# A sliding-window attention and Fourier mix: the two heads of a transposed score tile interleaved by row, so that one selection masks both

## The chip, the cores and the metric

The kernel runs on one core of one Trainium2 chip. The metric is the device time of one execution in microseconds (us); the kernel before and the changed kernel are each executed several times and the median is taken.

## The reference

Only `A_x` is used as the input of both branches (`B_x` is not read). Cut to what matters:

```python
# S = 2048 rows, D = 512, H = 32 heads of Dh = 16, window W = 256
x = A_x
g = sigmoid((x * gate_w).sum(-1, keepdims=True))

# branch a: Fourier mixing as real matrix products
a_ = x @ dft_hid_re.T ; b_ = x @ dft_hid_im.T
a  = dft_seq_re @ a_ - dft_seq_im @ b_

# branch b: causal attention over a sliding window of 256 keys
q, k, v = split_heads(x @ wqkv)
scores = (q @ k.T) * Dh ** -0.5
scores = where(0 <= i - j < W, scores, -1e9)
b = merge_heads(softmax(scores) @ v) @ wo

out = g * a + (1 - g) * b
```

## The kernel before

All products are taken in the type fp32r, and where full precision is wanted an operand is split into a high part `hi` and a rest `lo`, so that three matmuls stand for one product (`TERMS`).

**Attention.** The 32 heads are worked in 4 groups (`NG`) of 4 pairs (`NP`). A step `n` is one group and one block of 64 rows (`BQ`), so there are 4 x 32 = 128 steps (`N`). In `ring[0]` lie the queries and in `ring[1]` the keys of a group, all 2048 columns, with 96 partitions per pair and a few rows more for corrections. A matmul for one pair takes as its stationary operand a padded block, `pads[i][n % 2][:, p]`, 128 columns wide: `make_pad` copies 64 columns of the ring twice, each time multiplied by a column of `half` (1 in one head's partitions, 0 in the other's), so that columns 0 to 63 belong to head 0 of the pair and columns 64 to 127 to head 1.

- `s_pair(n, p)` (L346) forms the scores of 64 queries of both heads against up to 320 keys (`WIN`) in PSUM (tile name `s`), adds the mask and takes the row minimum on DVE (L358), then takes the exponential and its sum on ScalarE (L361). Only the minimum and the sum are kept.
- `t_pair(k, p)` (L426) runs `LAG` = 19 steps behind. It forms the transposed scores (tile name `t`): 64 keys of both heads on the partitions, up to 320 queries on the free axis, with the minimum already added by rows 96 to 99 of the operands. ScalarE takes the exponential into `pt` (L440). After every second pair GpSimd (POOL) sets the two ragged ends of the window to zero with affine selections: the first 64 columns (L445) and, for full windows, the last 64 (L449), for each head's 64 partitions by itself.
- `pv(n)` (L452) multiplies `pt` with `vpad`: for each pair 128 rows (64 keys of head 0, then 64 keys of head 1) by 32 columns, of which 16 belong to each head and the other 16 are zero. `v_load` (L406) brings the values of 4 steps from HBM into `vr`, `v_spread` (L416) copies them into the right quarter of `vpad` on POOL; the zeros were set once at the start (`clear_pads`, L203).
- `make_pad(0, ..)` runs on DVE for both heads, `make_pad(1, ..)`, the operand of `t_pair`, on DVE for head 0 (L339) and on ScalarE for head 1 (L337).

**Dense work.** The generator `dense()` yields matmuls of the projections (`dv`, `dqk`, `dab`) and of the two 2048 x 2048 products of the Fourier branch (`dc`, L518); `fill(n)` inserts them between the matmuls of the attention at a fixed rate, so that PE has work while DVE and ScalarE finish a score tile. DVE splits the DFT matrices as they arrive (L574, queued as `jobs`), DVE and ScalarE evict the PSUM tiles.

**Order.** PE's order is written out by hand (`manual_schedule`); the main loop at L836 sets which step of what stands where. `behind(...)` keeps some DVE, ScalarE and SP instructions in the order in which they are issued; the rest, POOL above all, is placed by a scheduler. Score tiles `s` and `t` share 4 PSUM buffers (`ps_a`): a matmul waits until the tile four places earlier was read by DVE (`s`) or by ScalarE (`t`). `pads[i]` has two buffers, `vpad` two, `vr` one.

**Start.** The first weights and the first quarter of x are split by DVE and ScalarE (L78 to L81, L157 to L159) before PE can form the first projection, while POOL builds the constants: `mask`, `ident`, `half`, `mrow`, the zero rows of `pads[0]` (L195) and of the rings (L191).

Of the kernel before, what the change touches and what calls it, by code (L numbers as in the profile page):

```python
# [7 lines left out]
F32 = mybir.dt.float32  # L8
F32R = mybir.dt.float32r
AF = mybir.ActivationFunctionType  # L10
OP = mybir.AluOpType
# [3 lines left out]
P = 128  # L15
# [5 lines left out]
BQ = 64  # L21
NB = S // BQ
WIN = 320
# [9 lines left out]
def fnet_window_mix(ctx: ExitStack, tc: tile.TileContext, xT, x, wqk, wv, wr, wi, cr, ci, wo, gw, out):  # L33
    nc = tc.nc

    const = ctx.enter_context(tc.tile_pool(name="const", bufs=1))
# [11 lines left out]
    v_scr = [dram.tile([2, P, 2, NG, 64], F32, name=f"v_scr{i}") for i in range(8)]  # L48
# [6 lines left out]
    def ld(dst, src):  # L55
        mark("sp", nc.sync.dma_start(dst, src))

    def f(ap):
        return ap.bitcast(F32)
# [4 lines left out]
    def mark(e, ins):  # L64
        last[e] = ins.ins

    @contextmanager
    def behind(*engines):
        with ExitStack() as es:
            for e in engines:  # L70
                if e in last:
                    es.enter_context(tc.issue_after(last[e]))
            yield
# [68 lines left out]
    with tc.manual_schedule(engines={mybir.EngineType.Activation, mybir.EngineType.DVE, mybir.EngineType.SP}):  # L142
# [12 lines left out]
        for dk in range(DK):  # L155
            c = slice(dk * 256, dk * 256 + 256)
# [7 lines left out]
    ring = [const.tile([P, NP, S], F32R, name=f"ring{i}") for i in range(2)]  # L164
# [3 lines left out]
    for h in (0, 64):  # L168
        m = mask[h:h + 64, :]
        nc.gpsimd.affine_select(m, m, pattern=[[1, WIN]], compare_op=OP.is_gt, fill=BIG,  # L170
                                base=0, channel_multiplier=-1)
        nc.gpsimd.affine_select(m, m, pattern=[[-1, WIN]], compare_op=OP.is_ge, fill=BIG,
                                base=256, channel_multiplier=1)
    ident = const.tile([P, P], F32R, name="ident")
    nc.gpsimd.memset(f(ident[:]), 1.0)
    nc.gpsimd.affine_select(ident[:], f(ident[:]), pattern=[[1, P]], compare_op=OP.is_equal, fill=0.0,
                            base=0, channel_multiplier=-1)

    half = const.tile([P, 2], F32, name="half")
    mrow = const.tile([P, 2], F32, name="mrow")  # L180
    for t, edges in ((half, ((0, 16, 32, 48, 64, 80), (16, 32, 48, 64, 80, 96))), (mrow, ((96, 98), (98, 100)))):
        nc.gpsimd.memset(t, 0.0)
        for h in range(2):
            for i, e in enumerate(edges[h]):
                a = t[:, h:h + 1]
                nc.gpsimd.affine_select(a, a, pattern=[[0, 1]], compare_op=OP.is_ge, fill=1.0 - i % 2,
                                        base=e - 1, channel_multiplier=-1)

    def clear_rows(i, ss):
        with behind("pool"):  # L190
            nc.gpsimd.memset(f(ring[i][96:128, :, ss * 512:(ss + 1) * 512]), 0.0)  # L191

    first_lo = f(XT[0, 0][96:128, 1]).rearrange("r (p c) -> r p c", p=NP)
    for t in pads[0]:
        mark("pool", nc.gpsimd.affine_select(t[96:128], first_lo, pattern=[[0, NP], [0, P]], compare_op=OP.is_gt,  # L195
                                             fill=0.0, base=0, channel_multiplier=0))
    clear_rows(1, 0)
    clear_rows(0, 0)
    vpad = [const.tile([P, 4, NP, 32], F32, name=f"vpad{b}") for b in range(2)]

    def clear_pads():
        for t in vpad:
            nc.gpsimd.memset(t, 0.0)  # L203
        for t in pads[1]:
            nc.gpsimd.memset(f(t[96:128]), 1.0)
            for h in range(2):
                a = t[96:128, :, 64 * h:64 * h + 64]
                nc.vector.tensor_scalar(a, f(a), mrow[96:128, h:h + 1], None, op0=OP.mult)


# [117 lines left out]
    def make_pad(i, n):  # L328
        if not 0 <= n < NG * NB:
            return  # L330
        t = pads[i][n % NPAD]
        b = n % NB
        with behind(*(("act", "dve") if n < NPAD else ())):
            for h in range(2):
                src, dst = f(ring[i][:96, :, b * BQ:(b + 1) * BQ]), t[:96, :, 64 * h:64 * h + 64]
                if i and h:
                    nc.scalar.activation(dst, src, AF.Copy, scale=half[:96, h:h + 1])  # L337
                else:
                    nc.vector.tensor_scalar(dst, src, half[:96, h:h + 1], None, op0=OP.mult)  # L339
        PAD[i, n] = t  # L340
# [65 lines left out]
    def v_load(n):  # L406
        if n >= NG * NB:
            return
        g, kb = divmod(n, NB)
        raw = at.tile([P, 4, 64], F32, name="vr", bufs=1)  # L410
        for h in range(2):
            ld(raw[64 * h:64 * h + 64].rearrange("r (c j) x -> r c j x", j=2),
               v_scr[kb // 4][:, :, h, g, :].rearrange("c (j r) x -> r c j x", r=64))
        VR[n] = raw

    def v_spread(n):  # L416
        if n >= NG * NB:
            return
        raw = VR.pop(n)
        v2 = vpad[n // 4 % 2]  # L420
        for h in range(2):
            r = slice(64 * h, 64 * h + 64)
            nc.gpsimd.tensor_copy(v2[r, :, :, 16 * h:16 * h + 16], raw[r].rearrange("r j (p d) -> r j p d", d=16))  # L423
        V2[n // 4] = v2

    def t_pair(n, p):  # L426
        q0 = n % NB * BQ
        w = min(WIN, S - q0)
        if p == 0:
            if "proj" in have:  # L430
                more.append(n)
            c = (n - more[0]) % 6 * NP * WIN if more else 3072
            if c + NP * WIN <= 3072:
                PT[n] = f(home[:, c:c + NP * WIN].rearrange("p (a b) -> p a b", a=NP))
            else:
                PT[n] = at.tile([P, NP, WIN], F32, name="pt", bufs=4)
        pt = PT[n]
        ps = ps_a.tile([P, 512], F32, name="t", tag="st")
        nc.tensor.matmul(ps[:, :w], PAD[1, n][:, p], ring[0][:, p, q0:q0 + w], start=True, stop=True)  # L439
        nc.scalar.activation(pt[:, p, :w], ps[:, :w], AF.Exp, scale=-1.0)  # L440
        if p % 2:
            ph = slice(p - 1, p + 1)
            for h in (0, 64):
                a = pt[h:h + 64, ph, 0:64]
                nc.gpsimd.affine_select(a, a, pattern=[[0, 2], [1, 64]], compare_op=OP.is_ge, fill=0.0,  # L445
                                        base=0, channel_multiplier=-1)
                if w == WIN:
                    a = pt[h:h + 64, ph, 256:320]
                    nc.gpsimd.affine_select(a, a, pattern=[[0, 2], [-1, 64]], compare_op=OP.is_gt, fill=0.0,  # L449
                                            base=0, channel_multiplier=1)  # L450

    def pv(n):  # L452
        g, kb = divmod(n, NB)
# [375 lines left out]
    def v_next(n):  # L829
        if n < N:  # L830
            for c in range(2):
                need(("v", n % NB // 2 + c))
            with behind(*(("sp",) if n < 8 else ())):
                v_load(n)

    for n in range(N + LAG + 1):  # L836
# [3 lines left out]
        if n == 7:  # L840
            clear_pads()
        k = n - LAG
        ring_ahead(n + 1)
        if k in (-1, 4):
            v_spread(0 if k < 0 else 4)
        if k in (-4, -1, 4):
            v_next({-4: 0, -1: 4, 4: 8}[k])
        if n == 0:
            make_pad(0, 0)
        for p in range(NP):  # L850
            if n < N:
                s_pair(n, p)
            fill(n)
            if 0 <= k < N:
                t_pair(k, p)
            if p == 0:
                make_pad(0, n + 1)
                if k >= -1:
                    make_pad(1, k + 1)
            fill(n)  # L860
            for at_n, at_p, do in TURN:
                u, j = divmod(n - at_n, 8)
                if p == at_p and j == 0 and 0 <= u < 16:
                    do(u)
            if p == 3 and k % 8 == 6 and 0 <= k < N:
                l_load(k // 8)
            if p == 0 and full:
                o_out()
            if p == 2 and (k - summed >= (5 if more else 3) or k == N):
                for j in range(summed, k):  # L870
                    pv(j)
                summed = k
            if p == 3 and 4 * spread - 5 < summed and 4 * spread < N and n >= fresh:
                v_spread(4 * spread)
                spread += 1
                v_next(4 * spread)
                fresh = n + 2
# [49 lines left out]
```

## Time and profile before

| what | value |
|---|---|
| time, median of 3 runs | 855.11 us (853.95 to 856.31) |
| profiled execution, its span | 854.1 us, 17219 instructions |
| PE matmul busy | 844.2 us, 99% of the span |
| DVE busy | 618.1 us, 72% |
| ScalarE (ACT) busy | 592.0 us, 69% |
| POOL busy | 372.6 us, 44%, 1067 instructions |
| DMA | 161.04 MB, mean 189 GB/s |

For the profiled execution the page gives the span, from its first to its last instruction, and no time beside it; the span lies 1.0 us below the median of the timed runs and within their range. In the page "busy" is the time in which an engine had an instruction under way; PE's matmuls are pipelined, so that a busy PE need not be at its peak. Each group's row reads: line, engine, operation, what it writes and reads with shapes, count, then busy us and mean ns of one, then the idle time of that engine just before these instructions and what ended most of it.

### The profile page before, as it was taken

How to read it: one execution, taken by the hardware profiler on the slowest of the kernel's cores; microseconds unless marked ns; L12 is line 12 of the kernel's file. 1: busy time of each engine (PE TensorE's matmuls, PEld its weight loads, DVE VectorE, ACT ScalarE, POOL GpSimd, SP SyncE). 2: the span in 40 equal slices, each digit the busy share in tenths (PEclk: the TensorE clock that was granted, in tenths of full speed). 3: DMA queues.
4: the chain of work that ended last, by engine and by line, in shares of the span. 5: the costliest groups of instructions: out<-in, count | busy, mean ns of one | idle time of the engine just before them, and what ended most of it. 6: DMA issues, size and time to landing. Idle time of an engine off the chain costs nothing.

```text
span 854.1 us, 17219 instructions
## 1 busy us (share of the span) xinstructions
PE 844.2 (99%) x5166; PEld 691.1 (81%) x5166; DVE 618.1 (72%) x2011; ACT 592.0 (69%) x1793; POOL 372.6 (44%) x1067
## 2 busy tenths in 40 slices
PE   8999999999999999999999999999999999999998
PEld 6788788788788888888878887788888887878876
DVE  5588978767879787669777787788988764447252
ACT  5388898888888987779778897678777765532020
POOL 9100254444542554555525555456355577830000
PEclk9999999999999999999999999999999999999999
DMA  7976577576665274444445447979784344339563
GB/s 240 289 234 201 177 253 239 203 240 216 205 233 188 52 221 129 145 121 151 138 133 143 158 150 228 267 264 298 246 232 136 119 154 133 130 119 289 148 188 133
DMA packets 94862, 161.04 MB, mean 189 GB/s; under 512 B 27312, under 2 KB 36272, under 8 KB 94768
## 3 DMA queue, kind: packets, MB, share of 16 engines
q1 hardware_dynamic: 94336, 159.28, 59.4%
q8 instruction: 40, 0.66, 0.3%
q10 hardware_dynamic: 432, 0.66, 0.2%
q14 instruction: 54, 0.44, 0.2%
HBM read 108.27 MB, written 51.64 MB: 187 GB/s over the span
## 4 chain that ended last, share of the span: by engine, by line
PE 92%; DVE 3%; DMA 3%; issue 1%; ACT 1%; SPq 0%; DVEq 0%; ACTq 0%
PE dc L518 40%; PE dab L294 10%; PE s L356 8%; PE t L439 8%; PE o L466 8%; PE dqk L271 8%; PE t L785 5%; PE dv L294 4%; DMA raw<-cr 1%; DMA raw<-xT 1%; DVE sm L358 1%; DMA pt<-wqk 1%; DVE pad L339 0%; DVE big L81 0%; DVE lo L574 0%
## 5 line engine op out<-in xcount | busy, mean ns | idle before, releaser
L361 ACT ACTIVATE sm<-sm,ml 128x320 f32<-128x320 f32 (+4 forms) x512 | 277.9, 544 | 102.7 <-DVE ml L358 97.3
L518 PE MATMUL dc<-big,hi 128*128 128x512 f32 x1020 | 344.1, 393 | 0.0
L358 DVE CUSTOM_DVE_ANT_0 sm<-s,mask 128x320 f32<-128x320 f32 (+4 forms) x512 | 235.3, 464 | 110.5 <-PE s L356 88.0
L445 POOL TENSOR_SCALAR_AFFINE_SELECT pt<-pt 64x128 f32<-64x128 f32 x392 | 136.1, 347 | 224.0 <-ACT pt L440 212.4
L518 PE MATMUL dc<-big,lo 128*128 128x512 f32 x510 | 200.5, 393 | 0.0
L518 PEld LDWEIGHTS dc<-big,hi 128*128 128x128 f32 x1020 | 179.7, 188 | 21.3
L440 ACT ACTIVATE pt<-t 128x320 f32<-128x320 f32 (+4 forms) x392 | 160.2, 411 | 43.5 <-PE t L439 41.1
L356 PE MATMUL s<-ring,pad 128*128 128x320 f32 (+4 forms) x512 | 157.7, 308 | 0.1
L439 PE MATMUL t<-ring,pad 128*128 128x320 f32 (+4 forms) x512 | 154.3, 301 | 0.4 <-DVE ml L358 0.4
L339 DVE TENSOR_SCALAR pad<-ring,half 96x256 fp32r<-96x256 f32 x384 | 119.8, 358 | 13.4 <-PE t L439 13.2
L449 POOL TENSOR_SCALAR_AFFINE_SELECT pt<-pt 64x128 f32<-64x128 f32 x344 | 121.7, 354 | 0.1
L356 PEld LDWEIGHTS s<-ring,pad 128*128 128x128 f32 x512 | 96.1, 188 | 30.2 <-issue 9.0
L439 PEld LDWEIGHTS t<-ring,pad 128*128 128x128 f32 x512 | 96.1, 188 | 22.4 <-DVE ml L358 1.6
L518 PEld LDWEIGHTS dc<-big,lo 128*128 128x128 f32 x510 | 95.9, 188 | 13.7 <-issue 1.6
L574 DVE TENSOR_TENSOR lo<-raw,hi 128x512 fp32r<-128x512 f32 x142 | 97.9, 698 | 0.1
L361 ACT ACTIVATION_READ_ACCUMULATOR sm<-sm,ml 128x1 f32 x512 | 97.5, 190 | 0.0
L294 PE MATMUL dab<-hi,big 128*128 128x512 f32 x256 | 89.1, 394 | 0.0
L271 PE MATMUL dqk<-big,hi 128*128 128x512 f32 x240 | 85.7, 394 | 1.3 <-DVE big L81 0.6
L423 POOL COPY vpad<-vr 64x256 f32<-64x256 f32 x64 | 26.9, 420 | 110.2 <-DMA vr<-v_scr 80.5
L574 DVE CAST hi<-raw 128x512 fp32r<-128x512 f32 x142 | 60.9, 438 | 17.4 <-PE dc L518 12.1
L445 POOL TENSOR_SCALAR_AFFINE_SELECT home<-home 64x128 f32<-64x128 f32 x120 | 45.1, 376 | 56.5 <-ACT home L440 49.0
L337 ACT ACTIVATE pad<-ring,half 96x256 fp32r<-96x256 f32 x128 | 63.8, 499 | 0.0
(96 smaller groups left out, 957.5 us busy)
## 6 DMA issues: line engine op xcount, KB each, us to landing
qk_scr<-home SPq DMA_DIRECT2D x32, 512.0 KB
ring<-qk_scr SPq DMA_DIRECT2D x32, 512.0 KB
raw<-cr SPq DMA_DIRECT2D x32, 512.0 KB
raw<-ci SPq DMA_DIRECT2D x32, 512.0 KB
r_scr<-ev SPq DMA_DIRECT2D x42, 256.0 KB
ev<-r_scr SPq DMA_DIRECT2D x42, 256.0 KB
ab_scr<-home SPq DMA_DIRECT2D x20, 512.0 KB
big<-ab_scr SPq DMA_DIRECT2D x20, 512.0 KB
```

What stands on the lines that cost most here:

```text
L271: nc.tensor.matmul(ps, w[a][:, c:c + 128], XT[dk, ss][:, b], start=n == 0, stop=n == 11)
L294: nc.tensor.matmul(ps, XT[dk, ss][:, a, c * 128:(c + 1) * 128], wh[b], start=n == 0, stop=n == 11)
L339: nc.vector.tensor_scalar(dst, src, half[:96, h:h + 1], None, op0=OP.mult)
L356: nc.tensor.matmul(ps[:, :w], PAD[0, n][:, p], ring[1][:, p, k0:k0 + w], start=True, stop=True)
L358: mark("dve", nc.vector.tensor_tensor_reduce(out=sm[:, :w], in0=ps[:, :w], in1=mask[:, WIN - w:], scale=1.0, scalar=3e38, op0=OP.add, op1= ...
L361: mark("act", nc.scalar.activation(sm[:, :w], sm[:, :w], AF.Exp, bias=nm[:, c], scale=-1.0, accum_out=l[:, c]))
L439: nc.tensor.matmul(ps[:, :w], PAD[1, n][:, p], ring[0][:, p, q0:q0 + w], start=True, stop=True)
L440: nc.scalar.activation(pt[:, p, :w], ps[:, :w], AF.Exp, scale=-1.0)
L445: nc.gpsimd.affine_select(a, a, pattern=[[0, 2], [1, 64]], compare_op=OP.is_ge, fill=0.0, base=0, channel_multiplier=-1)
L449: nc.gpsimd.affine_select(a, a, pattern=[[0, 2], [-1, 64]], compare_op=OP.is_gt, fill=0.0, base=0, channel_multiplier=1)
L518: nc.tensor.matmul(ps, w[a][:, i % 8 * 128:i % 8 * 128 + 128], ab[SC[i]][:, b], start=i == ends[0] and a + b == 0, stop=i == ends[1] and a ...
L574: return fn(*args)
```

## The change

In `pads[1]`, the operand of the transposed scores, the two heads of a pair no longer take columns 0 to 63 and 64 to 127 but alternate: column 2r + h is key r of head h. So the rows of `t` and `pt` alternate too, both heads' ragged ends lie in one pattern of rows and columns, and one affine selection over 128 partitions takes the place of two over 64. `make_pad(1, ..)` writes every second element on DVE and on ScalarE as before, in two instructions. The values have to follow: `v_load` fetches both heads' rows alternating with one DMA in place of two, and `v_spread` multiplies all 128 rows with a column that is 1 for one head's rows and 0 for the other's (`side`), so that the zeros of `vpad` are written each time and its clearing at the start goes. `side` is formed on DVE at the start from every second column of `ident`. The untransposed scores (`s`) keep their order.

```diff
@@ constants
+    side = const.tile([P, 2], F32, name="side")
 ...
+    nc.vector.reduce_sum(side[:, 0:1], f(ident[:]).rearrange("p (r h) -> p h r", h=2)[:, 0],
+                         axis=mybir.AxisListType.X)
+    nc.vector.tensor_scalar(side[:, 1:2], side[:, 0:1], -1.0, 1.0, op0=OP.mult, op1=OP.add)
+
+    def turned(t):
+        return t[:].rearrange("x p (r h) -> x p r h", h=2)
@@ clear_pads
-        for t in vpad:
-            nc.gpsimd.memset(t, 0.0)
         for t in pads[1]:
             nc.gpsimd.memset(f(t[96:128]), 1.0)
             for h in range(2):
-                a = t[96:128, :, 64 * h:64 * h + 64]
+                a = turned(t)[96:128, :, :, h]
                 nc.vector.tensor_scalar(a, f(a), mrow[96:128, h:h + 1], None, op0=OP.mult)
@@ make_pad
-                src, dst = f(ring[i][:96, :, b * BQ:(b + 1) * BQ]), t[:96, :, 64 * h:64 * h + 64]
+                src = f(ring[i][:96, :, b * BQ:(b + 1) * BQ])
+                dst = turned(t)[:96, :, :, h] if i else t[:96, :, 64 * h:64 * h + 64]
                 if i and h:
                     nc.scalar.activation(dst, src, AF.Copy, scale=half[:96, h:h + 1])
                 else:
@@ v_load
-        for h in range(2):
-            ld(raw[64 * h:64 * h + 64].rearrange("r (c j) x -> r c j x", j=2),
-               v_scr[kb // 4][:, :, h, g, :].rearrange("c (j r) x -> r c j x", r=64))
+        ld(raw.rearrange("r (c j) x -> r c j x", j=2),
+           v_scr[kb // 4].rearrange("c (j r) h g x -> g (r h) c j x", r=64)[g])
@@ v_spread
         for h in range(2):
-            r = slice(64 * h, 64 * h + 64)
-            nc.gpsimd.tensor_copy(v2[r, :, :, 16 * h:16 * h + 16], raw[r].rearrange("r j (p d) -> r j p d", d=16))
+            nc.gpsimd.tensor_scalar(v2[:, :, :, 16 * h:16 * h + 16], raw.rearrange("r j (p d) -> r j p d", d=16),
+                                    side[:, h:h + 1], None, op0=OP.mult)
@@ t_pair
         if p % 2:
             ph = slice(p - 1, p + 1)
-            for h in (0, 64):
-                a = pt[h:h + 64, ph, 0:64]
-                nc.gpsimd.affine_select(a, a, pattern=[[0, 2], [1, 64]], compare_op=OP.is_ge, fill=0.0,
-                                        base=0, channel_multiplier=-1)
-                if w == WIN:
-                    a = pt[h:h + 64, ph, 256:320]
-                    nc.gpsimd.affine_select(a, a, pattern=[[0, 2], [-1, 64]], compare_op=OP.is_gt, fill=0.0,
-                                            base=0, channel_multiplier=1)
+            a = pt[:, ph, 0:64]
+            nc.gpsimd.affine_select(a, a, pattern=[[0, 2], [2, 64]], compare_op=OP.is_ge, fill=0.0,
+                                    base=1, channel_multiplier=-1)
+            if w == WIN:
+                a = pt[:, ph, 256:320]
+                nc.gpsimd.affine_select(a, a, pattern=[[0, 2], [-2, 64]], compare_op=OP.is_gt, fill=0.0,
+                                        base=-1, channel_multiplier=1)
```

## Prediction

> **What bounds the kernel now.** I read the page's totals and its slices first, then who PE waited for, then stretches of 25 us.
>
> ```profile
> span 854.1 us, 17219 instructions
> PE 844.2 (99%) x5166; PEld 691.1 (81%) x5166; DVE 618.1 (72%) x2011; ACT 592.0 (69%) x1793; POOL 372.6 (44%) x1067
> ...
> PE   8999999999999999999999999999999999999998
> ...
> PEclk9999999999999999999999999999999999999999
> ...
> PE 92%; DVE 3%; DMA 3%; issue 1%; ACT 1%; SPq 0%; DVEq 0%; ACTq 0%
> ```
>
> PE has a matmul under way for 844.2 of 854.1 us, at the full clock in every slice, and the chain that ended last is 92% PE. A busy PE could still hide short waits, so the list of what PE waited for decides:
>
> ```profile
> PE t L785 <- DVE ev L787: 1.9, 1, 1.9
> PE dv L579 <- DVE ev L146: 1.5, 1, 1.5
> PE dqk L271 <- DVE big L81: 0.6, 1, 0.6
> PE dqk L271 <- DVE home L86: 0.6, 1, 0.6
> PE s L376 <- DVE mlh L370: 0.5, 1, 0.5
> ...
> PEld o L466 <- POOL home L445: 1.4, 4, 0.4
> ```
>
> The largest two lie at the two ends (a late addition of the output, the first zeroed tile) and have nothing to do with the change. Inside the attention PE waited 1.1 us for DVE in these rows, and its weight loads 1.4 us for POOL. The rest of the 854 us is PE's own work. Three stretches, with PE, PEld, DVE, ACT and POOL busy in that order:
>
> ```profile
> 275.00:300.00 25.00, 25.00 (x160) 20.23 (x158) 19.56 (x67) 23.05 (x71) 12.22 (x40) 1.00 0.32 84
> 625.00:650.00 25.00, 25.00 (x144) 20.91 (x146) 23.70 (x77) 20.86 (x65) 16.95 (x42) 1.00 0.67 201
> 725.00:750.00 25.00, 25.00 (x180) 20.62 (x179) 10.98 (x22) 14.24 (x34) 20.17 (x60) 1.00 0.40 133
> ```
>
> ACT at 23.05 of 25 and DVE at 23.70 of 25 held PE up in neither; POOL at 20.17, where only transposed scores are left, did not either. In the built program PE's order is the same, instruction for instruction, with the same shapes. So the change can win only what PE waits, and lose only what it makes PE wait.
>
> **Part 1: half the selections on POOL.**
>
> ```profile
> L445 POOL TENSOR_SCALAR_AFFINE_SELECT pt<-pt 64x128 f32<-64x128 f32 x392 | 136.1, 347 | 224.0 <-ACT pt L440 212.4
> L449 POOL TENSOR_SCALAR_AFFINE_SELECT pt<-pt 64x128 f32<-64x128 f32 x344 | 121.7, 354 | 0.1
> L423 POOL COPY vpad<-vr 64x256 f32<-64x256 f32 x64 | 26.9, 420 | 110.2 <-DMA vr<-v_scr 80.5
> L445 POOL TENSOR_SCALAR_AFFINE_SELECT home<-home 64x128 f32<-64x128 f32 x120 | 45.1, 376 | 56.5 <-ACT home L440 49.0 <-PE dc L518 2.7
> L449 POOL TENSOR_SCALAR_AFFINE_SELECT home<-home 64x128 f32<-64x128 f32 x104 | 39.3, 377 | 0.0
> L176 POOL TENSOR_SCALAR_AFFINE_SELECT ident<-ident 128x128 fp32r<-128x128 f32 x1 | 0.3, 292 | 0.1
> ...
> L445 POOL TENSOR_SCALAR_AFFINE_SELECT pt<-pt x392: 286/292/1140, 103.3 to 764.3; 64x128 f32<-64x128 f32 x196
> ```
>
> 960 selections (392 + 344 + 120 + 104) become 480 over 128 partitions. The one row with that shape, `ident`, took 292 ns, and the median over 64 partitions is also 292 ns: partitions cost nothing here, columns do. So POOL loses about 480 x 0.35 = 168 us of its 372.6. Nobody on the path gets that: POOL's idle time in front of L445 is 224.0 us, so a quicker pass ends in a longer wait for ScalarE. What PE can get back is the 1.4 us; its matching PE waits are not in the list, so I take -0.2, between -1.4 and 0.
>
> `v_spread` keeps 64 instructions, now over 128 partitions with a per-row factor. No row shows POOL multiplying by a column. The copy's 420 ns is one end; the other I put at twice that, 840 ns: 64 x 0.42 = 27 us more POOL work, inside the time just freed and a step or more ahead of the `pv` that reads it. Nothing on PE.
>
> `v_load` becomes one DMA of the same rows of 256 B: 32 fewer issues on SP's queue, the same bytes, and the value tile is fetched several steps ahead: nothing.
>
> **Part 2: the operand of the transposed scores is written with a step of two elements.** As many instructions as before, 128 on DVE (h = 0) and 128 on ScalarE (h = 1); the other 256 of L339's 384 are untouched.
>
> ```profile
> L339 DVE TENSOR_SCALAR pad<-ring,half 96x256 fp32r<-96x256 f32 x384 | 119.8, 358 | 13.4 <-PE t L439 13.2
> L574 DVE TENSOR_TENSOR lo<-raw,hi 128x512 fp32r<-128x512 f32 x142 | 97.9, 698 | 0.1
> ...
> L337 ACT ACTIVATE pad<-ring,half 96x256 fp32r<-96x256 f32 x128 | 63.8, 499 | 0.0
> L574 DVE CAST hi<-raw 128x512 fp32r<-128x512 f32 x142 | 60.9, 438 | 17.4 <-PE dc L518 12.1 <-DMA raw<-ci 3.8 <-DMA raw<-cr 1.5
> ...
> L361 ACT ACTIVATE sm<-sm,ml 128x320 f32<-128x320 f32 x448 | 250.6, 561 | 86.9 <-DVE ml L358 82.3
> ...
> L361 ACT ACTIVATE sm<-sm,ml 128x64 f32<-128x64 f32 x16 | 5.5, 346 | 2.3 <-DVE ml L358 2.2
> ```
>
> No row writes fp32 with such a step, so the cost has two ends. The lower is zero. For the upper on DVE I take the gap between a one-source and a two-source pass over 512 elements, 698 - 438 = 260 ns, so 130 ns for 256: what losing the double rate costs. On ScalarE the slope of L361 is (561 - 346) / 256 = 0.84 ns an element; every element at half rate adds 215 ns. Together 128 x (0.130 + 0.215) = 44 us of engine time at most; I expect a third of it, since only the written side changes.
>
> [...]
>
> Who would wait? ScalarE's pad write stands between two reads of score tiles:
>
> ```profile
> 300.96 0.31 PE L439 MATMUL t<-ring,pad 128*128 128x320 f32 x1
> ...
> 301.86 0.42 ACT L440 ACTIVATE pt<-t 128x320 f32<-128x320 f32 x1
> ...
> 303.38 0.31 PE L439 MATMUL t<-ring,pad 128*128 128x320 f32 x1
> ```
>
> The tile formed at 300.96 is read by 302.28; the matmul that takes over its buffer two places on starts at 303.38: 1.1 us of margin against at most 0.215 us. L445's starts run from 103.3 to 764.3, and in those 661 us there are 128 pads of each kind, 4.8 in 25 us: in the fullest stretches above that adds at most 4.8 x 0.130 = 0.6 us to DVE's 23.70 and 4.8 x 0.215 = 1.0 us to ACT's 23.05. Both still fit in 25. I take +0.3 us for steps in which an eviction and a pad meet, between 0 and +4.4 (a tenth of the 44 us).
>
> **Part 3: the start.**
>
> ```profile
> L203 POOL MEMSET vpad<- 128x512 f32 x2 | 1.2, 620 | 0.1
> ```
>
> ```profile
> 2.46 0.29 POOL L176 TENSOR_SCALAR_AFFINE_SELECT ident<-ident 128x128 fp32r<-128x128 f32 x1
> ...
> 4.35 0.43 DVE L80 CAST big<-pt 128x512 fp32r<-128x512 f32 x1 [2.88 <-DMA pt<-xT]
> ...
> 7.01 1.67 POOL L195 TENSOR_SCALAR_AFFINE_SELECT pad<-big 32x512 fp32r<-32x512 f32 x2
> 7.07 1.12 DVE L81 TENSOR_TENSOR big<-pt,big 128x512 fp32r<-128x512 f32 x1 [1.22 <-ACT big L78]
> ...
> 8.11 0.85 DVE L159 TENSOR_TENSOR lo<-pt,hi 128x256 fp32r<-128x256 f32 x1
> ...
> 8.88 0.68 DVE L81 TENSOR_TENSOR big<-pt,big 128x512 fp32r<-128x512 f32 x1
> ...
> 9.48 0.41 DVE L159 TENSOR_TENSOR lo<-pt,hi 128x256 fp32r<-128x256 f32 x1
> ...
> 24.88 1.29 DVE L81 TENSOR_TENSOR big<-raw,big 128x512 fp32r<-128x512 f32 x2
> 26.20 1.16 DVE L208 TENSOR_SCALAR pad<-pad,mrow 32x256 fp32r<-32x256 f32 x4
> ```
>
> The two instructions that form `side` stand on DVE ahead of its first cast and wait for `ident`, which is there at 2.75; the cast waits for its DMA until 4.35. Even at 0.5 us each they hide. The two `vpad` clears (1.2 us of POOL) go, so L195 starts up to 1.2 us earlier and no longer lies over the DVE passes at 7.07 and 8.11, which took 1.12 and 0.85 us where the same ones took 0.68 and 0.41 at 8.88 and 9.48. That frees at most 0.44 + 0.44 = 0.9 us ahead of PE's first projection. Against it, the built program puts one of the four L208 writes between the two L81 at 24.88, and PE's 0.6 us wait (`dqk` for `big` L81) ends with the second: 0.3 us later (1.16 / 4), or 0.6 with the step. I take -0.2, between -0.9 and +0.6.
>
> **Sum.** -0.2 - 0.2 + 0.3 = -0.1 on a span of 854.1: 854.0. The timed median lies 1.0 us above that span, so 855.0 us. About 0.3%, 2.6 us, is what a measurement of this kernel can tell from no change.
>
> **Rivals.**
> *Late readers (slower).* If a strided write costs more than the upper end, DVE is full at 625 us from 1.3 / 4.8 = 0.27 us a pad on, ACT at 275 us from 1.95 / 4.8 = 0.41; past that each pad pushes a read of a score tile over its margin, PE stands, and the dense matmuls behind it in its fixed order stand too. Priced at a tenth of 44 us with the start at its worst: +4.4 + 0.6 = 5.0, about 860. For it: no row excludes such a price. Against: 1.1 us of margin. [...]
> *Fewer collisions (faster).* POOL's selections have a median of 292 ns but a mean of 347 and a longest of 1140, and the DVE passes at 7.07 and 8.11 were stretched beside POOL. With half the selections DVE runs freer, and the waits for DVE and POOL inside the stream (0.6 + 0.6 + 0.5 + 1.4) and the 0.9 of the start go: -4.0, about 851. Against: most of the stretched passes hold up nobody. [...]
> *It does not halve POOL's work.* If 128 partitions cost twice 64, POOL stays at 372 us and PE as it is: 855 again. The `ident` row speaks against it.
>
> **Chances.** No change, with or without the halving: 0.70 (0.65 and 0.05). Late readers 0.17, fewer collisions 0.13. Hence faster 0.13, same 0.70, slower 0.17. The range runs from 852.0, short of the full -4.0, to 859.0, short of the full +5.0.
>
> **What would show it.** Right: POOL near 200 us, PE's list of waits as short as before, PE busy within 2 us of 844. Part 1 is wrong if a selection of 128x128 takes over 0.45 us; part 2 if L339's strided form takes over 0.6 us or waits of `s` and `t` for ACT or DVE appear in PE's list; part 3 if the first cast on DVE starts after 4.4 us. A span over 857 with PE's waits unchanged would overturn the claim that PE's own rate is untouched.

## The result, and the profile after

The changed kernel takes 867.4 us (median of 4 runs, 866.55 to 872.34); the kernel before, run beside it, 855.71 us (853.95 to 859.79). The ratio is 1.0134 [1.0094, 1.0174]: slower, and outside the predicted range. The profiled run took 867.15 us, with a span of 865.4.

The page's totals, PE's and the clock's slices and the chain of the changed kernel:

```profile
span 865.4 us, 16699 instructions
PE 856.5 (99%) x5166; PEld 694.0 (80%) x5166; DVE 615.6 (71%) x2013; ACT 595.8 (69%) x1793; POOL 248.8 (29%) x585
...
PE   9999999999999999999999999999999999999988
...
PEclk9999999999999999999999999999999999999999
...
PE 91%; DMA 5%; DVE 2%; issue 1%; ACT 1%; SPq 0%; ACTq 0%; DVEq 0%
```

POOL is down by 124 us as intended. But PE, with the same 5166 matmuls, is busy 12.3 us longer (844.2 before). What PE waited for, in the changed kernel:

```profile
PE t L790 <- DVE ev L792: 2.6, 1, 2.6
PE dv L584 <- DVE ev L146: 1.5, 1, 1.5
PE dqk L277 <- DVE home L86: 0.6, 1, 0.6
PE s L383 <- DVE mlh L377: 0.6, 1, 0.6
PE dab L300 <- DVE home L88: 0.3, 1, 0.3
PE s L265 <- DVE big L81: 0.2, 1, 0.2
...
PEld o L471 <- POOL pt L454: 1.4, 4, 0.4
```

The list is as short as before; no `s` or `t` waits for the changed pad writes or the selections. So PE doesn't stand longer; it takes longer for the same work. The costliest group of matmuls by line, of before and of after (busy us, mean ns of one):

```profile
L518 PE MATMUL dc<-big,hi 128*128 128x512 f32 x1020 | 344.1, 393 | 0.0
...
L518 PE MATMUL dc<-big,lo 128*128 128x512 f32 x510 | 200.5, 393 | 0.0
```

```profile
L523 PE MATMUL dc<-big,hi 128*128 128x512 f32 x1020 | 348.4, 397 | 0.0
...
L523 PE MATMUL dc<-big,lo 128*128 128x512 f32 x510 | 202.7, 398 | 0.0
```

The 512-column projection, whose instruction, shape and order the change did not touch, grew by 4 to 5 ns each. Where in the span? The matmuls that read `pad`, first of before, then of after (ns min/median/max, then first and last start in us):

```profile
L356 PE MATMUL s<-ring,pad x512: 191/310/418, 35.2 to 688.2; 128*128 128x320 f32 x149, 128*128 128x64 f32 x6, 128*128 128x256 f32 x6, 128*128 128x128 f32 x5
L439 PE MATMUL t<-ring,pad x512: 191/310/417, 100.9 to 763.5; 128*128 128x320 f32 x150, 128*128 128x128 f32 x6, 128*128 128x256 f32 x5, 128*128 128x192 f32 x5
```

```profile
L363 PE MATMUL s<-ring,pad x512: 192/312/422, 34.0 to 696.3; 128*128 128x320 f32 x149, 128*128 128x64 f32 x6, 128*128 128x256 f32 x6, 128*128 128x128 f32 x5
L445 PE MATMUL t<-ring,pad x512: 191/310/373, 100.3 to 772.5; 128*128 128x320 f32 x150, 128*128 128x128 f32 x6, 128*128 128x256 f32 x5, 128*128 128x192 f32 x5
```

These rows cut the span in three, and I use the cut below. The start (up to the first `s`) went from 35.2 to 34.0 us: -1.2. **The stretch of the attention**, from the first `s` to the last `t`, went from 763.5 - 35.2 = 728.3 to 772.5 - 34.0 = 738.5 us: +10.2. What follows it went from 90.6 to 92.9: +2.3. Together +11.3, the whole difference of the spans.

The +2.3 has its own place: PE's longest wait, in the last part (start us, duration; before, then after).

```profile
828.59 7.80 PE L785 MATMUL t<-fin,os 128*128 128x512 f32 x33 [1.90 <-DVE ev L787]
```

```profile
838.43 4.10 PE L790 MATMUL t<-fin,os 128*128 128x512 f32 x11 [2.60 <-DVE ev L792]
```

PE stood 2.6 instead of 1.9 us (+0.7), and the 11 matmuls after that took 4.10 / 11 = 0.37 us each against 7.80 / 33 = 0.24 before (+1.5). In the stretch from 838 to 842 us the granted clock was 0.69 (third number from the end); in the kernel before it was 1.00 from 828 to 840 us, behind that wait:

```profile
838.00:842.00 4.00, 3.56 (x11) 2.86 (x12) 2.36 (x4) 0.00 (x0) 0.00 (x0) 0.69 0.62 137
```

That wait was there before and differs from run to run: run e1 below, the same instructions with `side` in another place, has 1.4 us there. The 10.2 us of the attention are what has to be explained. There the clock is full (1.00 from 45 to 690 us), PE is busy throughout, and its distances from one start to the next have grown. I worked these out from the start times in the trace. Summed over the whole stretch, the distances from a dense 512-column matmul to the score matmul behind it grew by 6.0 us, those from a score matmul to the next dense one by 1.2, and those from that one to a second dense one by 2.8: 10.0 of the 10.2 us.

The same per group: take a score matmul of 320 columns with the dense one before it and the one behind it, from the start of the first to the start of what follows the last. As a mean between 45 and 690 us (some 380 to 410 groups of each kind in a run; at most five of over 0.7 us are left out) a group with `s` took 602.3 ns before and 612.1 after, one with `t` 602.2 and 615.4. Between 775 and 825 us, where only dense matmuls run, the median distance of two of them is 0.227 us in both kernels. One such matmul is under way for 393 or 397 ns in the rows above, so the next starts before it ends.

### The profile page after: what moved, and what is told of

It reads as the page before. It is cut to its first block, busy times and chain, and to the rows that moved or that the text cites. A ratio compares the mean times of both kernels' runs of the same rounds, so it can differ in the third digit from the quotient of the medians.

```text
span 865.4 us, 16699 instructions
## 1 busy us (share of the span) xinstructions
PE 856.5 (99%) x5166; PEld 694.0 (80%) x5166; DVE 615.6 (71%) x2013; ACT 595.8 (69%) x1793; POOL 248.8 (29%) x585
## 4 chain that ended last, share of the span: by engine, by line
PE 91%; DMA 5%; DVE 2%; issue 1%; ACT 1%; SPq 0%; ACTq 0%; DVEq 0%
PE dc L523 40%; PE dab L300 10%; PE s L363 9%; PE t L445 8%; PE dqk L277 8%; PE o L471 8%; PE dv L300 5%; PE t L790 2%; DMA out<-ev 2%; DMA ev<-o_scr 1%; DMA qk_scr<-home 1%; DMA pt<-wqk 1%; PE s L265 0%; DVE sm L365 0%; DVE os L81 0%
## 5 line engine op out<-in xcount | busy, mean ns | idle before, releaser
L523 PE MATMUL dc<-big,hi 128*128 128x512 f32 x1020 | 348.4, 397 | 0.0
L523 PE MATMUL dc<-big,lo 128*128 128x512 f32 x510 | 202.7, 398 | 0.0
L450 POOL TENSOR_SCALAR_AFFINE_SELECT pt<-pt 128x128 f32<-128x128 f32 x196 | 70.9, 362 | 309.9 <-ACT pt L446 308.4
L428 POOL TENSOR_SCALAR vpad<-vr,side 128x256 f32<-128x256 f32 x64 | 61.1, 966 | 126.7 <-DMA vr<-v_scr 77.5
L579 DVE CAST hi<-raw 128x512 fp32r<-128x512 f32 x142 | 59.8, 430 | 17.0 <-PE dc L523 12.3
L344 ACT ACTIVATE pad<-ring,half 96x256 fp32r<-96x256 f32 x128 | 66.6, 520 | 0.0
L454 POOL TENSOR_SCALAR_AFFINE_SELECT pt<-pt 128x128 f32<-128x128 f32 x172 | 60.7, 353 | 0.1
L446 ACT ACTIVATE home<-t 128x320 f32<-128x320 f32 (+4 forms) x120 | 49.0, 408 | 15.3 <-PE t L445 12.8
```

Source lines behind the costliest of these rows:

```text
L450: nc.gpsimd.affine_select(a, a, pattern=[[0, 2], [2, 64]], compare_op=OP.is_ge, fill=0.0, base=1, channel_multiplier=-1)
L523: nc.tensor.matmul(ps, w[a][:, i % 8 * 128:i % 8 * 128 + 128], ab[SC[i]][:, b], start=i == ends[0] and a + b == 0, stop=i == ends[1] and a ...
L579: return fn(*args)
```

## The theories

- **Address.** The change adds one tile, `side`, behind `mrow`. It holds 8 bytes in each partition, occupies 32, and moves every tile allocated later by 32 bytes: `big`, `hi`, `lo`, `raw`, `vpad`, the score tiles. `pads`, the rings, `ident`, `half` and `mrow` stay. PE then reads the same data from other places, and slower.
- **New work.** The strided pads, the spread by a factor or the 128-partition selections hold PE up in some way that the list of waits does not show.
- **Chip.** The chip or the hour, not the kernel.

## Experiments

Time ratios are to the kernel before, run beside on the same chip. The stretch is the attention's, in the run with the profile, as worked out above.

**e1: all the new work, the old addresses.** `side` is put into the slot that `mrow` already has.

```
-    mrow = const.tile([P, 2], F32, name="mrow")
-    side = const.tile([P, 2], F32, name="side")
+    mrow4 = const.tile([P, 4], F32, name="mrow")
+    mrow, side = mrow4[:, 0:2], mrow4[:, 2:4]
```

> The changed kernel, with the column side kept in the free bytes behind mrow instead of in a tile of its own, so that every SBUF tile lies at the address that it has in the kernel before (the tile of its own moves all tiles behind it by 32 bytes). Theory A, the address: the 32 bytes make PE's matmuls slower beside the other engines; this kernel returns to about 855 us and the median distance of two 512-column matmuls in the attention from 0.2315 to 0.228 us. Theory B, the new work (strided pads, spread by a multiplication, fewer selections): stays at about 867 us. Theory C, the chip or its clock on the day: time goes with the chip and not with the kernel, so all four kernels of this job lie within 0.5% of each other.

**e2: none of the new work, the new addresses.** The kernel before with an unused tile.

```
     mrow = const.tile([P, 2], F32, name="mrow")
+    side = const.tile([P, 2], F32, name="side")
+    nc.gpsimd.memset(side, 0.0)
```

> The kernel before with one unused tile of 8 bytes behind mrow, zeroed once on POOL: nothing else changes, but all later SBUF tiles move by 32 bytes, as in the changed kernel. Theory A (address): about 866 us, distance of 512-column matmuls 0.2315 us. Theory B (new work): about 855 us and 0.228 us. Theory C (chip): as the other kernels of this job.

**e3, e4: the changed kernel and the kernel before again**, beside e1 and e2.

> The changed kernel as it is, once more beside the kernel before. Theories A and B: about 1.3% over the kernel before, 867 us, 0.2315 us between 512-column matmuls in the attention. Theory C (chip): within 0.5% of the kernel before.

> The kernel before, timed against itself, and its profile on this chip. Theories A and B: about 855 us and 0.228 us between 512-column matmuls. Theory C (chip): if the chip sets the rate, 0.231 us or more here too.

Measured: e1 855.92 us, 1.0005 [0.9983, 1.0028]; e2 865.05 us, 1.0113 [1.0082, 1.0144]; e3 869.5 us, 1.0161 [1.0115, 1.0207]; e4 857.55 us, 1.0023 [1.0004, 1.0043]. The page's totals and the pad rows of e1, then the same of e2:

```profile
PE 845.6 (99%) x5166; PEld 692.6 (81%) x5166; DVE 615.9 (72%) x2013; ACT 593.3 (69%) x1793; POOL 252.1 (29%) x585
```

```profile
L363 PE MATMUL s<-ring,pad x512: 191/310/419, 38.6 to 692.0; 128*128 128x320 f32 x149, 128*128 128x64 f32 x6, 128*128 128x256 f32 x6, 128*128 128x128 f32 x5
L445 PE MATMUL t<-ring,pad x512: 191/310/414, 104.4 to 767.2; 128*128 128x320 f32 x150, 128*128 128x128 f32 x6, 128*128 128x256 f32 x5, 128*128 128x192 f32 x5
```

```profile
PE 854.8 (99%) x5166; PEld 692.0 (80%) x5166; DVE 618.6 (72%) x2011; ACT 594.8 (69%) x1793; POOL 368.9 (43%) x1068
```

```profile
L358 PE MATMUL s<-ring,pad x512: 191/312/422, 35.8 to 697.3; 128*128 128x320 f32 x149, 128*128 128x64 f32 x6, 128*128 128x256 f32 x6, 128*128 128x128 f32 x5
L441 PE MATMUL t<-ring,pad x512: 191/310/393, 101.8 to 773.6; 128*128 128x320 f32 x150, 128*128 128x128 f32 x6, 128*128 128x256 f32 x5, 128*128 128x192 f32 x5
```

e1 has all of the change (POOL at 252.1, 585 instructions) and the old stretch, 767.2 - 38.6 = 728.6. e2 has nothing of the change but an idle 32-byte slot, and the new stretch, 773.6 - 35.8 = 737.8. The address theory stands; new work is refuted. e3 and e4, on the same chip, repeat their kernels, so the chip is out. The kernel before came out 0.23% above itself in e4, so a difference of that size says nothing here.

**Which tiles?** e5 moves only the pool of the score tiles (`pt`, `sm` and the like) by 32 bytes. e6 moves the dense operands the other way (-32) and leaves the score tiles (`vpad` and `home` move by +32). e7 drops a 64-byte tile, so that all later ones stand 64 bytes lower. e8 is e7 with the tiles from `sm` on 32 bytes off.

```
# e5, e6: ahead of the pool of score tiles
+    gap = ctx.enter_context(tc.tile_pool(name="gap", bufs=1)).tile([P, 2], F32, name="gap")
 ...
+    nc.gpsimd.memset(gap, 0.0)
# e6, e7, e8: one 64-byte tile fewer (e6 also has side behind mrow, as e2)
-            e = const.tile([P, 16], F32, name="ge")
+            e = gl
# e8: ahead of sm
+        if n == 0 and p == 0:
+            nc.gpsimd.memset(at.tile([P, 8], F32, name="gap", bufs=1), 0.0)
```

> The kernel before with 32 unused bytes in front of the pool at alone: pt, ml, sm, mlh, mhl and vr lie 32 bytes further on, everything PE reads in the dense matmuls stays. Theory A1 (ScalarE's and DVE's score tiles sm and pt off a 64-byte line slow PE): about 865 us, 0.2315 us between 512-column matmuls. Theory A2 (PE's own operands big, hi and lo off a line): 855 us, 0.228 us.

> The other half: vpad, gl, g1, g0 and home move by +32 bytes, big, hi, lo, raw and ev by -32 bytes (the tile ge is dropped, its value written over gl, to make room), and the pool at lies where it lay. Theory A1 (score tiles): 855 us, 0.228 us. Theory A2 (PE's operands): about 865 us, 0.2315 us between 512-column matmuls. If both halves matter, each is in between.

> All pools behind the constants move by -64 bytes (the tile ge is dropped, its value written over gl). If what matters is the place inside a 64-byte line: 855 us and 0.228 us. If it is the address itself, the distance to the unmoved rings and pads or a longer line: another time, up to 866 us.

> As the kernel moved by -64 bytes, with 32 bytes put between ml and sm: sm, mlh, mhl and vr lie off a 64-byte line, pt and everything else on one. Theory A1 with sm alone as the cause: about 865 us and 0.2315 us already from 50 us on. With pt as the cause: 855 us. Theory A2 (PE's operands): 855 us.

Measured: e5 856.54 us, 1.0011 [0.9994, 1.0028]; e6 860.38, 1.0048 [1.0023, 1.0072]; e7 864.29, 1.0091 [1.0069, 1.0113]; e8 867.76, 1.0129 [1.0105, 1.0153]. The score tiles by themselves change next to nothing (e5: 1.1 us of stretch), the dense operands do (e6), and moving by 64 bytes hurts too (e7), so the place inside 64 bytes does not decide. e8 lies 2 us of stretch (738.8 against 736.8) and 3.5 us of median above e7, though only the tiles from `sm` on differ; what that is stays open.

**Own place, or place against each other?** The attention's matmuls load `pad` and stream `ring`; the dense ones between them load and stream `big`, `hi`, `lo`. e9 moves all of these together by 32 bytes (a tile ahead of `pads`). e10 and e11 leave the dense operands and move `pads` and rings up by 32 and 64 bytes instead, by allocating `half` (and `mrow`) ahead of them: as far apart as in e6 and e7, at other addresses.

```
# e9
+    gap = const.tile([P, 2], F32, name="gap")
     pads = [[const.tile([P, NP, P], F32R, name=f"pad{i}_{b}") for b in range(NPAD)] for i in range(2)]
 ...
+    nc.gpsimd.memset(gap, 0.0)
# e10: half ahead of pads; e11: half and mrow
+    half = const.tile([P, 2], F32, name="half")
     pads = [[const.tile([P, NP, P], F32R, name=f"pad{i}_{b}") for b in range(NPAD)] for i in range(2)]
 ...
-    half = const.tile([P, 2], F32, name="half")
```

> The kernel before with 32 unused bytes ahead of everything: pads, rings, constants and all pools move together by +32 bytes. Theory D (what counts is where the operands of the attention, pads and rings, lie against those of the dense matmuls, big, hi and lo, since PE loads the weights of the one while it streams the other): nothing changes against each other, so 855 us and 0.228 us between 512-column matmuls. Theory E (what counts is each tile's own address): about 865 us and 0.2325 us.

> Only pads, rings, mask and ident move by +32 bytes (the tile half is placed ahead of them); big, hi, lo, home and the pool at keep their addresses. Theory D: as where the dense operands moved by -32, about 860 us, with the last dense matmul before a score matmul at 0.232 us where it took 0.227. Theory E with the dense operands: 855 us.

> The same with 64 bytes (half and mrow ahead of the pads). Theory D: as where the dense operands moved by -64, about 864 us and 0.233 us. Theory E with the dense operands: 855 us.

Measured: e9 860.02 us, 1.0044 [1.0027, 1.006]; e10 863.4, 1.0089 [1.0066, 1.0112]; e11 864.66, 1.0105 [1.009, 1.012]. The pad rows of e9, e7 and e11:

```profile
L358 PE MATMUL s<-ring,pad x512: 191/310/418, 40.1 to 693.1; 128*128 128x320 f32 x149, 128*128 128x64 f32 x6, 128*128 128x256 f32 x6, 128*128 128x128 f32 x5
L441 PE MATMUL t<-ring,pad x512: 191/310/416, 105.8 to 768.8; 128*128 128x320 f32 x150, 128*128 128x128 f32 x6, 128*128 128x256 f32 x5, 128*128 128x192 f32 x5
```

```profile
L356 PE MATMUL s<-ring,pad x512: 192/308/417, 35.9 to 696.9; 128*128 128x320 f32 x149, 128*128 128x64 f32 x6, 128*128 128x256 f32 x6, 128*128 128x128 f32 x5
L439 PE MATMUL t<-ring,pad x512: 192/305/374, 101.3 to 772.7; 128*128 128x320 f32 x150, 128*128 128x128 f32 x6, 128*128 128x256 f32 x5, 128*128 128x192 f32 x5
```

```profile
L356 PE MATMUL s<-ring,pad x512: 192/309/417, 35.2 to 696.5; 128*128 128x320 f32 x149, 128*128 128x64 f32 x6, 128*128 128x256 f32 x6, 128*128 128x128 f32 x5
L439 PE MATMUL t<-ring,pad x512: 192/305/392, 100.7 to 772.6; 128*128 128x320 f32 x150, 128*128 128x128 f32 x6, 128*128 128x256 f32 x5, 128*128 128x192 f32 x5
```

e9's stretch is 768.8 - 40.1 = 728.7, that of before, with every operand at another address. e7's is 736.8 and e11's 737.4: different addresses, the same distance, the same loss; their groups of three matmuls agree within 0.1 ns (table), e6's and e10's within 0.3. So, for the moves tried, the **distance** between the attention's operands and the dense ones decides, not the address of either. e9 is nevertheless 0.44% slower in time. In its profile that lies wholly ahead of the attention, which starts at 40.1 instead of 35.2 us: PE's wait for `big` L81 is 3.0 us there instead of 0.6, and the granted clock is 0.50 from 28 to 32 us, behind it. The mean granted clock of its five runs was 0.995 to 0.999, that of the runs beside it 0.999 to 1.000. Why this start waited longer stays open.

**How far, and which of the two?** The same means, other distances: e12 (+128), e15 (+96), e16 (+160), e14 (+192) place more of the small tiles (`half`, `mrow`, `gl`, `g1`) ahead of `pads` (`vpad`, allocated between, moves by 64 or 128 bytes with them). e13 places two of them between `pads` and rings, so that only the rings move by 64; e17 puts the rings first, so that only `pads` move by 64 against the dense operands; both also move by whole multiples of 8192 bytes.

> The same with 128 bytes (half, mrow and gl ahead of the pads; vpad moves by +64). Theory D with a period of 128 bytes: 855 us and 0.228 us as in the kernel before. Theory D with a longer period: another value, above or below. Theory E with the dense operands: 855 us.

> The kernel before with half and mrow between the pads and the rings: rings, mask and ident move by +64 bytes; the pads, which PE loads as weights, and all dense operands stay. Theory D1 (the loading of a pad collides with the streaming of the dense operand before it): the last dense matmul before a score matmul keeps its 0.227 us, the time is within 0.3% of 855. Theory D2 (the streaming of a ring collides with the loading of the dense weights behind it): the distances after a score matmul grow, and with them the first dense matmul; 860 to 865 us.

> The kernel before with pads, rings, mask and ident moved by +192 bytes (half, mrow, gl and g1 ahead of them); the dense operands stay. If only the place inside 128 bytes counted, this would be as +64: 864 us. With a longer period it is a value of its own; a group of two dense matmuls and a score matmul, 0.604 us in the kernel before, could lie between 0.597 (no collision left) and 0.615.

> The same with +96 bytes (half and gl ahead). Within 128 bytes this is the distance of the changed kernel mirrored (its dense operands moved by +32). Theory D: not the 855 us of the kernel before but 858 to 866, with 0.229 to 0.235 us for the last dense matmul before a score matmul. Theory E: 855 us.

> The same with +160 bytes (half, gl and g1 ahead). Period of 128 bytes: as +32, 863 us. Longer period: a value of its own, 850 to 866 us.

> The kernel before with the rings placed ahead of the pads (both by whole multiples of 8192 bytes) and half and mrow between them, so that the pads alone move by +64 bytes against rings and dense operands. Where the rings alone moved by 64 the time rose by 0.5%, where pads and rings moved together by 1.05%. If the two add up: another 0.5%, about 860 us, a group of two dense matmuls and a score matmul at 0.609 us against 0.604. If the pads do nothing by themselves: 855 us and 0.604 us.

All runs by distance of `pads` and rings from the dense operands, counted from the kernel before. The groups are those with `s` and with `t` described above, in ns.

| distance, bytes | run | group s / t, ns | stretch, us | median, us | ratio [95%] |
|---|---|---|---|---|---|
| 0 | before (first profile) | 602.3 / 602.2 | 728.3 | 855.71 | |
| 0 | e4 | 602.2 / 601.9 | 727.9 | 857.55 | 1.0023 [1.0004, 1.0043] |
| 0 | e1 | 602.7 / 602.7 | 728.6 | 855.92 | 1.0005 [0.9983, 1.0028] |
| 0 | e18 (below) | 602.3 / 602.9 | 728.3 | 856.32 | 1.0002 [0.9977, 1.0027] |
| 0 | e9 | 602.9 / 602.8 | 728.7 | 860.02 | 1.0044 [1.0027, 1.006] |
| 0, score tiles +32 | e5 | 603.6 / 603.9 | 729.4 | 856.54 | 1.0011 [0.9994, 1.0028] |
| -32 | after | 612.1 / 615.4 | 738.5 | 867.4 | 1.0134 [1.0094, 1.0174] |
| -32 | e3 | 612.3 / 614.9 | 738.0 | 869.5 | 1.0161 [1.0115, 1.0207] |
| -32 | e2 | 612.4 / 615.3 | 737.8 | 865.05 | 1.0113 [1.0082, 1.0144] |
| +32 | e6 | 607.8 / 607.4 | 733.0 | 860.38 | 1.0048 [1.0023, 1.0072] |
| +32 | e10 | 607.9 / 607.7 | 735.7 | 863.4 | 1.0089 [1.0066, 1.0112] |
| +64 | e7 | 613.0 / 614.1 | 736.8 | 864.29 | 1.0091 [1.0069, 1.0113] |
| +64 | e11 | 613.0 / 614.2 | 737.4 | 864.66 | 1.0105 [1.009, 1.012] |
| +64, `sm` off | e8 | 614.9 / 615.5 | 738.8 | 867.76 | 1.0129 [1.0105, 1.0153] |
| +96 | e15 | 610.2 / 611.8 | 736.8 | 862.9 | 1.0069 [1.0042, 1.0095] |
| +128 | e12 | 606.0 / 609.4 | 732.0 | 858.7 | 1.0045 [1.0028, 1.0062] |
| +160 | e16 | 612.1 / 612.0 | 736.0 | 866.65 | 1.0104 [1.0068, 1.0139] |
| +192 | e14 | 605.2 / 604.8 | 731.1 | 858.5 | 1.0024 [0.9999, 1.005] |
| rings +64 | e13 | 608.4 / 608.9 | 733.5 | 860.44 | 1.0051 [1.0027, 1.0075] |
| `pads` +64 | e17 | 608.3 / 610.4 | 734.5 | 861.51 | 1.0054 [1.0029, 1.0078] |

Three readings. Both operands take part: the 0.51% of the rings (e13) and the 0.54% of `pads` (e17) add up in time to the 1.05% of both (e11); in the groups they come to a little more (12 and 15 ns against 11 and 12). e17 rests on the multiples of 8192 bytes counting for nothing, which no run tests by itself. Neither of the two theories named for e13 holds alone: over the stretch, the mean distance around `s` grew in front of the score matmul (228.2 to 230.6 ns) and between the two dense ones behind it (234.1 to 236.7). The loss neither grows with the distance nor comes back every 128 bytes (+128 differs from 0, +160 from +32). And among the distances tried none is better than that of the kernel before. (e10's stretch is 2.7 us above e6's at equal groups: its profile also has 2.0 us of waits of `t` on DVE.)

**e18: the change, with the distance kept.** `side` is allocated ahead of `pads`, so everything moves by the same 32 bytes.

```
+    side = const.tile([P, 2], F32, name="side")
     pads = [[const.tile([P, NP, P], F32R, name=f"pad{i}_{b}") for b in range(NPAD)] for i in range(2)]
 ...
-    side = const.tile([P, 2], F32, name="side")
```

> The changed kernel with the tile side placed ahead of the pads instead of behind mrow: all tiles move by the same 32 bytes and keep their distances. Theory D (distance between the operands of the attention and of the dense matmuls): the 1.3% go, 855 to 858 us, and the work of the change itself costs nothing measurable. Theory B (the new work costs the time): 867 us.

Measured: 856.32 us, 1.0002 [0.9977, 1.0027]. Its page's totals and dense group, then its pad rows:

```profile
PE 844.3 (99%) x5166; PEld 691.8 (81%) x5166; DVE 615.0 (72%) x2013; ACT 593.2 (70%) x1793; POOL 253.1 (30%) x585
...
L523 PE MATMUL dc<-big,hi 128*128 128x512 f32 x1020 | 344.0, 393 | 0.0
```

```profile
L363 PE MATMUL s<-ring,pad x512: 191/310/418, 33.9 to 687.0; 128*128 128x320 f32 x149, 128*128 128x64 f32 x6, 128*128 128x256 f32 x6, 128*128 128x128 f32 x5
L445 PE MATMUL t<-ring,pad x512: 191/310/411, 99.7 to 762.2; 128*128 128x320 f32 x150, 128*128 128x128 f32 x6, 128*128 128x256 f32 x5, 128*128 128x192 f32 x5
```

PE is back at 844.3 us and 393 ns a matmul, POOL stays at 253.1, and the stretch is 728.3. Moving one allocation line takes the changed kernel back to the time of before. No version tried beats the kernel before.

Two rivals are only in part answered. The loss might come from other engines that read or write the same tiles. Between 700 and 760 us, where DVE is busy for 28 and ScalarE for 31 to 32 of 60 us, against about 80% each from 45 to 690 us, a group with `t` in the changed kernel still loses 13 ns (601.1 to 614.1, in the fuller part 602.2 to 615.4); but at +64 (e7, e11) it loses there only about half of its 12 ns. So other engines are not needed for the changed kernel's loss, but their part is not ruled out. And the place of the score tiles has a smaller effect of its own (e8 against e7).

Open: what in the memory or in PE's two operand reads makes the distance count, whether it repeats at a larger distance, and whether a distance not tried is faster. In every mixed group where the loss shows, two matmuls with operands from the two sets of tiles overlap (the next weights are loaded while one streams: in the changed kernel PEld is under way for 694.0 us and PE for 856.5 of 865.4); that this is the mechanism is argued, not shown.

## Why the prediction was wrong

The step that failed is the last sentence on the bound: "the change can win only what PE waits, and lose only what it makes PE wait." It held that the same matmuls in the same order cost the same. The new tile `side` was costed by the two instructions that fill it, and not by what stands behind it in memory. The 10.2 us of the attention came through that gap, and e2 shows that this tile alone brings 1.13% [0.82, 1.44]. The prediction's own test, a span over 857 with PE's waits unchanged, is what came.

The rest of the steps, with the rows of the changed kernel:

```profile
L450 POOL TENSOR_SCALAR_AFFINE_SELECT pt<-pt 128x128 f32<-128x128 f32 x196 | 70.9, 362 | 309.9 <-ACT pt L446 308.4 <-DMA qk_scr<-home 1.4
L428 POOL TENSOR_SCALAR vpad<-vr,side 128x256 f32<-128x256 f32 x64 | 61.1, 966 | 126.7 <-DMA vr<-v_scr 77.5 <-PE o L471 27.7 <-issue 11.0
L454 POOL TENSOR_SCALAR_AFFINE_SELECT pt<-pt 128x128 f32<-128x128 f32 x172 | 60.7, 353 | 0.1
L450 POOL TENSOR_SCALAR_AFFINE_SELECT home<-home 128x128 f32<-128x128 f32 x60 | 26.9, 448 | 86.6 <-ACT home L446 84.0 <-PE dc L523 2.6
L454 POOL TENSOR_SCALAR_AFFINE_SELECT home<-home 128x128 f32<-128x128 f32 x52 | 18.1, 348 | 0.0
```

*Part 1* was right on the selections: 480 of them, 70.9 + 60.7 + 26.9 + 18.1 = 176.6 us against 342.2, so -165.6 where -168 was forecast, and the time went into a longer wait for ScalarE (224.0 to 309.9 us). The spread costs 966 ns, above the upper end of 840: +34 us of POOL instead of +27, hidden as forecast. POOL came to 248.8, not "near 200"; that figure had left out the spread, since the part's own terms make 372.6 - 168 + 27 = 232. Of the remaining 17 us, 10 are the spread and the selections; most of the rest is that POOL's rows overlap by 12 us in place of 20, which the page's total counts once. The 1.4 us of waits for POOL, of which I took 0.2 as gain, did not move.

```profile
L346 DVE TENSOR_SCALAR pad<-ring,half 96x256 fp32r<-96x256 f32 x384 | 119.1, 356 | 14.8 <-PE t L445 14.6
L344 ACT ACTIVATE pad<-ring,half 96x256 fp32r<-96x256 f32 x128 | 66.6, 520 | 0.0
```

*Part 2:* the written step costs nothing on DVE (356 ns against 358; the row holds 256 untouched passes as well, but of the three passes of one step, two of them untouched, none stands out: 346, 343 and 345 ns at 164.9 us) and 21 ns on ScalarE (520 against 499), a tenth of its upper end; nobody waited. So the late readers did not come: slower was right only in sign, by another mechanism. The upper end on DVE was an estimate from the pace of a pass with one source against that of a pass with two. In the kernel before:

```profile
L81 DVE TENSOR_TENSOR big<-raw,big 128x512 fp32r<-128x512 f32 x12 | 8.1, 689 | 3.3 <-ACT big L78 3.3
...
L370 DVE TENSOR_TENSOR mlh<-ml,mlh 128x64 fp32r<-128x64 f32 x16 | 4.0, 250 | 0.2
L369 DVE CAST mlh<-ml 128x64 fp32r<-128x64 f32 x16 | 3.6, 223 | 0.0
...
L80 DVE CAST big<-raw 128x512 fp32r<-128x512 f32 x8 | 3.3, 424 | 6.7 <-DMA raw<-xT 6.7
```

From 64 to 512 elements the casts grow by (424 - 223) / 448 = 0.45 ns an element, the passes with two sources by (689 - 250) / 448 = 0.98, about twice as much. That a step on the written side would cost DVE this difference was the author's assumption; the 356 ns do not bear it out.

*Part 3:* the first rows of the changed kernel's timeline (start us, duration):

```profile
2.72 0.22 DVE L190 TENSOR_REDUCE side<-ident 128x1 f32<-128x64 f32 x1 [1.27 <-POOL ident L176]
2.98 0.15 DVE L192 TENSOR_SCALAR side<-side 128x1 f32<-128x1 f32 x1
...
4.34 0.45 DVE L80 CAST big<-pt 128x512 fp32r<-128x512 f32 x1 [1.21 <-DMA pt<-xT]
```

`side` hides behind the first DMA, as forecast. The first `s` starts 1.2 us earlier in this profile (-0.2 was taken), but that start lies between 33.9 and 40.1 us in the runs above, e1's at 38.6 with the same instructions: more than the term can be measured by. The two DVE passes that lay under POOL's took 0.98 and 0.41 us in place of 1.12 and 0.85, so 0.6 of the 0.9 us came, too little to be seen in the times of e1 and e18. With the address shift taken out (e1, e18), the measured ratios are 1.0005 and 1.0002: the forecast of no change was right for the work that it counted.

## What to carry to other kernels

One added 8-byte tile moved the tiles allocated after it by 32 bytes, and in this kernel, which PE bounds, that alone cost 1.1% (e2): compare the tile addresses of both versions before reading a difference as the cost of the new work. The sign to look for is PE busy for longer on matmuls that were not touched (here 856.5 against 844.2 us), at full clock and with no new waits. Then two runs settle it: the old kernel with the new layout, and the new kernel with the old layout.

## What the runs showed of the hardware

- PE's rate in this kernel changed with how far apart the operands of neighbouring matmuls lie in memory: 602 to 604 ns for a group of three at the distance of before, 605 to 616 at the other distances tried, at steps of 32 bytes. PE's list of waits shows no new one in the changed kernel, and yet a group took 10 to 13 ns longer there.
- A wait of PE of 2.6 us (L790, above) was followed by matmuls at 0.37 instead of 0.24 us, under a granted clock of 0.69 in that stretch; a wait of 2.5 us at the same line in e18 was not: its 48 matmuls after that took 11.24 us, 0.23 each. Here the wait cost 1.5 us more behind it, over half of its own length again. The length of the longest wait does not tell by itself: the mean granted clock of the profiled execution was 0.998 in e8 and in e10, where that wait took 2.0 us (L787) and 2.1 us (`big` L81), and 1.000 in e2 and in e3, where it took 2.4 us (L787) and 2.3 us (`big` L81).
- On POOL, partitions were free: the median selection of 128x128 took 294 ns and that of 64x128 had taken 292. Columns were not: a selection of 64x320 (`mask`, L170) took 448.
